# A step order for attention and a gated feed-forward layer on one core: another order of the compute steps, an earlier zeroing, the last output block in three column pieces

## The chip, the core and the metric

The kernel runs on one core of a Trainium2 chip. Five engines work side by side, each through its own list of instructions in order: TensorE (PE) multiplies matrices and writes to PSUM, VectorE (DVE) and ScalarE (ACT) do the elementwise work, GpSimd (POOL) and SyncE (SP) issue most transfers. An instruction starts when the one before it on its engine has gone and the semaphores that it waits for have been counted up. The metric is the device time of one execution in microseconds (us); lower is better.

## What is computed

Block-sparse attention over 32 heads of 768 tokens, then a feed-forward layer with a depthwise convolution as gate. Cut to what matters:

```python
# q, k, v: [4, 8, 768, 64]; mask from blocks of 32 tokens: neighbours, first and last, 3 sampled ones per row
scores = np.where(mask, q @ k.T / 8.0, -1e9)            # per batch and head
attn = softmax(scores)
x = (attn @ v).transpose(0, 2, 1, 3).reshape(4, 768, 512)
h = np.maximum(x @ w_in, 0.0)                            # [4, 768, 1024]
conv_out = sum(conv_w[k] * shifted(h, k - 1) for k in range(3))   # along the tokens
out = (h * sigmoid(conv_out)) @ w_out                    # [4, 768, 512]
```

## The kernel before

**Tiles.** Heads are taken in pairs P = 0 to 15. K and Q of a pair are brought to a transposed slot `t` of 88 rows: 64 rows of the head dimension and 24 rows that carry the block mask, so that one matmul gives masked scores. Pairs 0 to 5 are transposed on PE (`k_tr`, `q_tr`) and copied out of PSUM (`k_cp`, `q_cp`, on DVE or ACT); later pairs are transposed by transfers on SP (`xb`) and copied by `stg_cp`. V gets a column of ones, set by the memsets `v_one`, and is cast or copied by `v_cp`.

**Stages.** The scores are cut into 144 units of eight 128x128 blocks. For each unit there are two `s` steps on PE (L762, into one of two PSUM buffers `st`), one `exp` on ACT (L774, 128x1024, from `st` into one of six buffers `pt`; the first unit's is cut in two halves, so that unit u has `exp.(u+1)` from the second unit on), and two `av` steps on PE (L799, eight matmuls of 65 columns). Counting from 0, unit u has `s.(2u)`, `s.(2u+1)`, `av.(2u)` and `av.(2u+1)`. When a pair's sums are complete, DVE takes the reciprocals and normalises (`rcp`, `norm`, L709), and X is transposed by a transfer (`x_xb`) or on PE (`x_tr`, `x_cp`). Then come x @ w_in on PE (`f1`, L896), `relu` (ACT L916 or DVE L918), the convolution and gate (`mul`, `add`, `g1`, `g2` on DVE, `tanh` on ACT; the last segment's convolution on PE with diagonal weights `diag`), and the second matmul (`f2`, L831), four steps of two matmuls to a block of 128 tokens, an eviction `ev` (ACT L327 or DVE L331) and an output transfer `out` (SP, L840). There are 24 such blocks; the last one (in the function `out_block`, `last`) is computed in column pieces into `st` buffers, which the scores no longer need by then.

**The start.** K, Q and V of pair 0 come as fp32 through the queues of SP and ACT; `cast_q` and `cast_k` bring them to bf16. The mask rows are built on DVE (`a1`, `a3`, `a4`, `a5`, with `ident` from POOL and the sampled blocks from a transfer) and copied into the slot by `m_q0`, `m_k`, `m_h1`, `m_q1`, `m_r1`, and into the other slots by `m_slot`. Until real work is there, PE runs 13 `warm` matmuls of 256 columns on a zeroed tile (`warm_mem`) and 32 `fill` matmuls of 128 columns, which stand at fixed places in its order. `he_zero` sets two edge columns of each of the two h tiles to zero (two memsets each, L364 and L365). The loads of later pairs and of the weights are issued on POOL (L239), held back by one-element `pace` copies.

**What sets the order.** Each step is entered in a graph with its dependences. The text `ORDER` then gives the order in which all steps are put down: two characters are a step's number (base 64), then a letter for its engine where it has a choice (A for ACT, V for DVE), then one character for each buffer that it takes. `put_down` reads it and issues the steps, with `tc.manual_schedule()`. An engine's list is the order in which its steps stand in that text. Costs and due times in the graph are not used when the order is given.

## Time and profile before

| | |
|---|---|
| runs of the kernel before | 207.41, 207.2, 208.66 us; median 207.41 |
| span of the profiled execution (first to last instruction) | 205.4 us |
| instructions | 6237 |
| granted TensorE clock, mean of the span | 1.000 |
| transfers | 25.59 MB, mean 125 GB/s |

The span is counted on the core from the first to the last instruction; the time of a run has some 2 us more around it. Busy times of an engine count each moment once, while the mean length of an instruction is from its start to its end, and neighbours overlap: the distance from one start to the next is what an instruction takes from the engine. A row of the timeline merges neighbours of a kind: start, duration, engine, line, operation, output and input, how many. In brackets stands the idle time before it and what ended it. Some matmul records are missing from the trace.

### The profile page before, as it was taken

The page shows a single profiled execution, that of the slowest core. Times are in us where ns is not written, and L with a number is a line of the kernel's source. Part 1 is how long each engine was busy: PE and PEld are TensorE (multiplying, and loading weights), DVE is VectorE, ACT ScalarE, POOL GpSimd, SP SyncE. Part 2 cuts the span into 40 slices and gives each one's busy share as a digit, 9 for nine tenths or more (in the row PEclk, how much of TensorE's full clock was granted, in tenths as well). Part 3 has the DMA queues.
Part 4 walks back from the last instruction along what each step waited for, and adds up shares of the span by engine and source line. Part 5 has one row for each costly group of instructions (what it writes and reads, how often), then busy time and mean ns, then how long its engine had stood idle before and what let it go on. Part 6 is the DMA issues. An engine that isn't in the chain of part 4 may idle for free.

```text
span 205.4 us, 6237 instructions
## 1 busy us (share of the span) xinstructions
PE 197.1 (96%) x2392; PEld 142.3 (69%) x2409; DVE 184.9 (90%) x572; ACT 189.7 (92%) x253; POOL 59.4 (29%) x113
## 2 busy tenths in 40 slices
PE   7799999999999999999999999999999999999992
PEld 5677877786667766776667767766567667787760
DVE  7999999999999998999899996999999959999960
ACT  6799999999999999999999998999999978998841
POOL 8689255312831133202443253900000000000000
PEclk9999999999999999999999999999999999999999
DMA  5999999994999979999779799998053131000405
GB/s 155 196 190 154 186 178 114 197 127 88 154 150 126 125 103 138 218 166 163 95 105 226 97 117 123 175 154 126 14 174 88 21 123 51 3 2 3 153 3 204
DMA packets 50969, 25.59 MB, mean 125 GB/s; under 512 B 36764, under 2 KB 47996, under 8 KB 50940
## 3 DMA queue, kind: packets, MB, share of 16 engines
q0 software_dynamic: 19728, 11.05, 46.0%
q1 hardware_dynamic: 30924, 13.86, 31.0%
q8 instruction: 19, 0.31, 0.6%
q10 hardware_dynamic: 288, 0.30, 0.5%
q14 instruction: 10, 0.08, 0.1%
HBM read 23.09 MB, written 6.29 MB: 143 GB/s over the span
## 4 chain that ended last, share of the span: by engine, by line
PE 68%; ACT 15%; DVE 12%; issue 3%; ACTq 0%; DVEq 0%
PE st L762 22%; PE mix L896 15%; PE mix L831 15%; PE av L799 12%; ACT pt L774 11%; DVE m L954 3%; DVE t L331 2%; DVE m L962 2%; ACT m L1001 1%; DVE xtok L709 1%; PE st L831 1%; ACT vt L327 1%; DVE diag L379 1%; ACT hE L916 1%; PE mix L728 1%
## 5 line engine op out<-in xcount | busy, mean ns | idle before, releaser
L774 ACT ACTIVATE pt<-st 128x1024 bf16<-128x1024 f32 (+1 forms) x145 | 142.2, 1051 | 4.2 <-PE st L762 3.7
L762 PE MATMUL st<-t 88*128 88x256 bf16 (+2 forms) x600 | 90.5, 267 | 2.3 <-DVE t L331 1.2
L799 PEld LDWEIGHTS <-pt 128*128 128x128 bf16 x1152 | 54.0, 97 | 14.2
L762 PEld LDWEIGHTS <-t 88*128 88x128 bf16 x600 | 48.9, 97 | 21.0 <-issue 1.9
L799 PE MATMUL av<-vt,pt 128*128 128x65 bf16 x1152 | 60.5, 193 | 0.1
L896 PE MATMUL mix<-xT,winb 128*128 128x384 bf16 (+2 forms) x288 | 55.2, 307 | 0.1
L954 DVE TENSOR_SCALAR m<-hE,cw 128x382 bf16<-128x382 bf16 (+2 forms) x192 | 49.1, 312 | 0.4 <-ACT hE L916 0.2
L831 PE MATMUL mix<-woutb,gT 128*128 128x512 bf16 x167 | 47.2, 379 | 0.7
L962 DVE TENSOR_TENSOR m<-m 128x764 bf16<-128x764 bf16 (+2 forms) x64 | 34.1, 532 | 0.6
L896 PEld LDWEIGHTS <-winb 128*128 128x128 bf16 x288 | 24.0, 97 | 9.2 <-issue 0.6
L1001 ACT ACTIVATE m<-m 128x764 bf16<-128x764 bf16 (+2 forms) x32 | 27.1, 853 | 0.0
L831 PEld LDWEIGHTS <-gT 128*128 128x128 bf16 x200 | 17.1, 97 | 10.0 <-DVE gT L1009 1.2
L407 POOL COPY pace<-pt 1x1 bf16<-1x1 bf16 x24 | 6.4, 268 | 54.1 <-ACT pt L774 54.0
L916 ACT ACTIVATE hE<-mix 128x384 bf16<-128x384 f32 (+2 forms) x39 | 19.8, 519 | 0.4 <-PE mix L896 0.2
L1009 DVE TENSOR_TENSOR gT<-m,hE 128x764 bf16<-128x764 bf16 (+3 forms) x36 | 18.2, 509 | 0.4
L709 DVE TENSOR_TENSOR xtok<-av,rcp 128x384 bf16<-128x384 f32 (+2 forms) x36 | 18.3, 507 | 0.4
L239 POOL DMA_DIRECT2D nat<-in_q_dram x23 | 17.3, 752 | 3.8 <-DMA nat<-in_k_dram 1.6
L918 DVE TENSOR_SCALAR hE<-mix 128x384 bf16<-128x384 f32 x25 | 13.7, 553 | 4.3 <-PE mix L896 3.7
L331 DVE COPY t<-mix 64x384 bf16<-64x384 bf16 (+1 forms) x33 | 13.2, 411 | 0.6 <-PE mix L460 0.2
L239 POOL DMA_DIRECT2D nat<-in_k_dram x15 | 12.0, 803 | 3.0 <-issue 2.4
L1004 DVE TENSOR_SCALAR m<-m 128x764 bf16<-128x764 bf16 (+3 forms) x36 | 11.9, 334 | 0.7 <-ACT m L1001 0.7
L327 ACT COPY o2s<-mix 128x512 f32<-128x512 f32 x15 | 9.2, 613 | 3.3 <-PE mix L831 3.2
(76 smaller groups left out, 118.2 us busy)
## 6 DMA issues: line engine op xcount, KB each, us to landing
out_dram<-o2s SPq DMA_DIRECT2D x23, 256.0 KB, 2.2
nat<-in_k_dram POOLq DMA_DIRECT2D x15, 192.0 KB, 4.5
vn<-in_v_dram POOLq DMA_DIRECT2D x15, 192.0 KB, 5.0
nat<-in_q_dram POOLq DMA_DIRECT2D x6, 192.0 KB, 4.5
winb<-in_moe_w_in_dram POOLq DMA_DIRECT2D x2, 512.0 KB, 8.4
woutb<-in_moe_w_out_dram POOLq DMA_DIRECT2D x4, 256.0 KB, 5.8
nat<-in_q_dram POOLq DMA_DIRECT2D x9, 96.0 KB, 5.1
nq<-in_q_dram POOLq DMA_DIRECT2D x6, 96.0 KB, 5.3
```

Of the source, the lines that this page charges most:

```text
L239: return op(name, {eng: occ}, lambda e: on(e).dma_start(out=dst(), in_=src), prio, deps, dma=(kind, service), **kw)
L709: nm = op("norm", {"DVE": t_dps(128 * C)}, lambda e: nc.vector.tensor_tensor(out=xtok_t[xk.index][:, 0:C].rearrange("p c h d -> p h c d"), ...
L762: nc.tensor.matmul(out=st[:, 128 * x:128 * (x + n_)], lhsT=t[0:88, 12 + 6 * hh + kc, :], rhs=t[0:88, idx:idx + (n_ - 1) * (2 if P < NPE el ...
L774: nc.scalar.activation(out=pt_t[ptb.index][:, c0:c1], in_=st_t[stb.index][:, c0:c1], func=AF.Exp, bias=0.0, scale=0.125)
L799: nc.tensor.matmul(out=o[:, off:off + 65], lhsT=pt_t[ptb.index][:, 128 * x:128 * x + 128], rhs=V_t[vslot_b[P].index][:, hh, kc, 0:65], sta ...
L831: nc.tensor.matmul(out=acc(), lhsT=gT_t[gb.index][:, ffc, 128 * t:128 * t + 128], rhs=woutb[:, ffc, c0:c1], start=(ffc == 0), stop=(ffc == ...
L896: nc.tensor.matmul(out=mix_t[hb.index][:, w1 * y:w1 * y + w1], lhsT=winb[:, fc, 128 * ffc:128 * ffc + 128], rhs=xT_t[xt_buf[n].index][:, f ...
L916: nc.scalar.activation(out=dst, in_=src, func=AF.Relu, bias=0.0, scale=0.5)
L954: nc.vector.tensor_scalar(out=m_t[cb.index][:, x, y, 0:w], in0=hE_t[heb.index][:, f0 + y, t0 + x:t0 + x + w], scalar1=cw[:, x, f0 + y:f0 + ...
L962: nc.vector.tensor_tensor(out=m[:, a_, :, 0:w], in0=m[:, a_, :, 0:w], in1=m[:, b_, :, 0:w], op=ALU.add)
L1001: th = [op("tanh", {"ACT": t_act(2 * w) + 0.04}, lambda e, cb=cb, w=w: nc.scalar.activation(out=m_t[cb.index][:, 0, :, 0:w], in_=m_t[cb.in ...
L1009: nc.vector.tensor_tensor(out=gT_t[gtb.index][:, f0:f0 + 2, t0:t1], in0=m_t[cb.index][:, 0, :, 0:w], in1=hE_t[heb.index][:, f0:f0 + 2, 1 + ...
```

## The change

Three things change in the text of the kernel.

1. `ORDER` is another text. All 1,787 steps of the old one are there, with six more (below). 37 steps have another engine, many buffers have another number, and within PE, ACT and DVE most steps stand at another place, by up to 27 places on PE, 8 on ACT and 70 on DVE. On POOL and SP transfers stay within five places of where they were.

Decoded, the beginning of two engines' lists (a digit after the dot counts the steps of a name):

```
DVE before: warm_mem v_one.3 ident_mem a1 nblk v_one.1 a3 ident24 m_k.0 m_h1.1 cast_q.0 a4 v_one.2 v_one.0
            a5.0 q_cp.0 m_q0.1 k_cp.3 cast_q.1 v_one.4 a5.1 m_h1.0 m_q1 m_r1 m_slot.0 k_cp.4 k_cp.5 q_cp.5 q_cp.4
DVE after:  he_zero.0 v_one.3 warm_mem v_one.0 ident_mem a1 nblk ident24 v_one.1 m_k.0 a3 a4
            a5.0 q_cp.0 a5.1 v_one.2 m_h1.1 k_cp.3 m_q1 m_h1.0 v_one.4 m_r1 m_slot.0 v_cp.0 k_cp.4 q_cp.5 k_cp.5
ACT before: m_k.1 cast_k.0 cast_k.1 k_cp.0 m_q0.0 k_cp.1 k_cp.2 exp.0 exp.1 q_cp.1 v_cp.0 exp.2 exp.3 exp.4
ACT after:  m_k.1 cast_q.0 cast_k.0 cast_k.1 k_cp.0 k_cp.1 m_q0.0 m_q0.1 cast_q.1 k_cp.2 exp.0 exp.1 q_cp.1
            exp.2 exp.3 q_cp.4 exp.4
```

On PE, six `fill` stand ahead of the first transpose `k_tr.0` before, one after; `s.0` and `s.1` had 12 `fill` ahead of them and now have 10 and 12, and the rest of the 32 are spread up to `s.16` in both. The steps with another engine:

```
DVE to ACT: cast_q.0 cast_q.1 m_q0.1 q_cp.4 q_cp.11 q_cp.16 relu.9 .11 .16 .18 .20 .24 .32 .39 v_cp.13 ev.15 ev.17 x_cp.7 ev.24
ACT to DVE: v_cp.0 relu.6 .12 .17 .19 .22 .28 .36 .37 .42 ev.1 .4 .6 .7 .21 .23 x_cp.4 x_cp.6
```

On POOL `pace.25` and `ld_win.0` change places, and so do some later paces with their neighbours; on SP some `x_xb` with some `xb`.

2. `he_zero.0`, the zeroing of the edge columns of one h tile, is the first step on DVE (part of the same text). Before, it stood behind the first normalisations.

3. The last output block has three pieces of columns, 256, 128 and 128, in place of two of 256. Each piece has its own four `f2` steps, its eviction and its output transfer, so there are six steps more. The last steps of each engine:

```
PE before:  .. f2.92 f2.96 f2.88 f2.86 f2.93 f2.89 f2.90 f2.94 f2.95 f2.91 f2.97 f2.98 f2.99 f2.87 f2.80 .81 .82 .83
PE after:   .. f2.88 f2.92 f2.96 f2.86 f2.89 f2.97 f2.93 f2.94 f2.98 f2.95 f2.90 f2.91 f2.87 f2.100 f2.99
            f2.101 f2.102 f2.103 f2.80 .81 .82 .83
SP before:  .. out.22 out.24 out.23 out.21 out.20
SP after:   .. out.22 out.24 out.25 out.23 out.21 out.20
```

(`f2.92` to `.95` are the first piece, `f2.96` to `.99` the second, `f2.100` to `.103` the third, which takes the `st` buffer of the first; `ev.20` and `out.20` belong to `f2.80` to `.83`.)

The diff, cut to its first and last lines of `ORDER`:

```diff
 ORDER = """
-000211g010M030405060708090a0S0T1T01U230251262h12j20U0L0O0N0P0Q0R0b0c0d0e0f0g0h0i0j0k0W1e0V0X12V13A17V1AV30Y1CA
...
-q/r0r1A0r2
+0M0L0S1i1g001d021010N0O0U0T03041T00P050W060Q071U080R0X1e090a12V13A2300b0c0d0V1AA10e2521CA0f0Y1DA1E1261K00Z0g1FA0
...
+rF1rL1rs3qQrtrR0r5ruqWrx0rDrGrSryrzrErMqXrNrTqYrOrHrPV0rIr6rJA2rX1rUrYrZrVArKr+qZ1r/VrWr7V3q+s0q/rQr0r8r1A1r2
 """
...
     def out_block(b, t, due, deps, after, tail=False, last=False):
         gb, ob = gt_buf[b], Buf(P_os)
-        halves = ((0, 256), (256, 512)) if last else ((0, 512),)
+        halves = ((0, 256), (256, 384), (384, 512)) if last else ((0, 512),)
...
-                due + 3, [evo], uses=[ob], dma=("hw", 0.65 if not last else 0.4)))
+                due + 3, [evo], uses=[ob], dma=("hw", {512: 0.65, 256: 0.4, 128: 0.25}[c1 - c0])))
```

77 lines of the change are left out of this document (38 added, 39 removed).

## The prediction

> **What bounds the kernel now.** I read the page first, then the busy time by stretch, then the start in order of time.
>
> ```profile
> PE 197.1 (96%) x2392; PEld 142.3 (69%) x2409; DVE 184.9 (90%) x572; ACT 189.7 (92%) x253; POOL 59.4 (29%) x113
> ...
> PE 68%; ACT 15%; DVE 12%; issue 3%; ACTq 0%; DVEq 0%
> ```
>
> Three engines are over 90% busy, and two thirds of the chain that ended last is TensorE (PE). Each row so far is an average, so the stretches come next.
>
> ```profile
> core 0: us, PE busy (x) PEld busy (x) DVE busy (x) ACT busy (x) POOL busy (x), PEclk, DMA share, GB/s
> 7.00:20.00 13.00, 12.37 (x178) 10.09 (x179) 12.40 (x33) 12.80 (x18) 10.47 (x18) 1.00 1.26 174
> 20.00:190.00 170.00, 168.54 (x2083) 121.57 (x2097) 158.72 (x484) 164.91 (x212) 42.74 (x83) 1.00 0.79 119
> ```
>
> From 20 to 190 us PE is busy 168.54 of 170 us: 1.46 us idle. ScalarE (ACT) is idle 5.09 us there and VectorE (DVE) 11.28. So PE bounds this stretch, and no order of the same matmuls can win more than 1.46 us in it. From 7 to 20 us ACT is busy 12.80 of 13 us while PE has gaps: there the exps set the pace. In the long stretch one wait on PE is on record:
>
> ```profile
> PE mix L728 <- DVE xtok L709: 0.3, 1, 0.3
> ```
>
> The 0.3 us are those of a transpose on a normalised block; no step waits for an exp. So what an order can still win lies mostly ahead of 20 us, and what it can lose lies anywhere that PE comes to wait.
>
> What sets the start is seen on DVE, then ACT:
>
> ```profile
> 1.82 0.55 DVE L286 COPY nblk<-ident 24x768 bf16<-24x768 bf16 x1
> ...
> 3.83 0.35 DVE L331 COPY t<-t 24x768 bf16<-24x768 bf16 x1
> ...
> 4.22 0.53 DVE L331 CAST nat<-o2s 128x192 bf16<-128x192 f32 x1
> ...
> 4.78 0.53 DVE L299 SCALAR_TENSOR_TENSOR A<-sbi,keyid,A 24x24 f32<-24x24 int32 x2
> ...
> 5.41 0.12 DVE L359 MEMSET vt<- 128x12 bf16 x2
> ...
> 5.57 0.61 DVE L299 SCALAR_TENSOR_TENSOR mtok<-sbi,keyid,A 24x384 bf16<-24x384 int32 x1
> ...
> 6.59 0.28 DVE L331 COPY t<-mtok 24x128 bf16<-24x128 bf16 x1
> ```
>
> ```profile
> 2.97 0.70 ACT L327 COPY t<-nblk 24x384 bf16<-24x384 bf16 x1
> 3.69 1.07 ACT L327 CAST nat<-o2s 128x384 bf16<-128x384 f32 x2
> 4.67 0.47 ACT L327 COPY t<-mix 64x384 bf16<-64x384 bf16 x1
> 6.21 0.40 ACT L327 COPY t<-mtok 24x256 bf16<-24x256 bf16 x1 [1.08 <-DVE mtok L299]
> 6.64 0.47 ACT L327 COPY t<-mix 64x384 bf16<-64x384 bf16 x1
> 7.29 0.47 ACT L327 COPY t<-av 64x384 bf16<-64x384 bf16 x1 [0.18 <-DVE t L331]
> 7.67 1.07 ACT L774 ACTIVATE pt<-st 128x512 bf16<-128x512 f32 x2
> 8.63 0.47 ACT L327 COPY t<-av 64x384 bf16<-64x384 bf16 x1
> 9.13 0.83 ACT L327 CAST vt<-m 128x768 bf16<-128x768 f32 x1
> 9.87 3.76 ACT L774 ACTIVATE pt<-st 128x1024 bf16<-128x1024 f32 x4
> ```
>
> The columns are start, duration, engine, line and operation. DVE goes without a pause through the casts and the mask to the mask rows `a5.0` (mtok, end 6.18). ACT has stood 1.08 us for them; `m_q0.0` starts at 6.21, and the first exp at 7.67. Then come two half exps, the copy `q_cp.1` and the cast of V, `v_cp.0`; the third exp starts at 9.87, and the exps after it start 0.90 apart ((3.76 − 1.06)/3, with the mean of one exp, 1.06, quoted below).
>
> **The change, part by part.** The start first. Ahead of `a5.0` DVE loses `m_h1.1` (start to next start, 3.83 to 4.22: 0.39), `cast_q.0` (4.22 to 4.78: 0.56) and the two `v_one` memsets (5.41 to 5.57: 0.16). One of those goes to the front (about 0.07), with the zeroing of the edge columns `he_zero.0`, which is two memsets like this:
>
> ```profile
> L364 DVE MEMSET hE<- x2: 65/65/65, 26.1 to 29.9; 128x8 bf16 x2
> ```
>
> Its two lines take 65 ns each, 0.13. Sum: 0.39 + 0.56 + 0.16 − 0.07 − 0.13 = 0.91, so `a5.0` ends near 5.27, if the sampled blocks are there when `a4` wants them at 3.9 instead of 4.78. The trace shows no wait that would bound their landing from below; `cast_k.0`, whose load was issued as early as any, ran unhindered at 3.69, so I take it that up to 0.3 could be lost, hidden by what follows. At the front of DVE the zeroing and one `v_one` delay the zeroed operand of the warm-up matmuls by about 0.2, and ident with it; ident is wanted by `nblk` (start 1.82, perhaps 2.0) and by POOL's first load, which waits behind it on POOL with all later loads, 0.2 each. ACT is shielded by its table load up to 2.97.
>
> ACT now becomes the longer way. After `m_k.1` (end 3.69) stand `cast_q.0` (half the elements of a `cast_k`, so between half of and all of 0.51; I take 0.33), the two `cast_k` (1.07 with overlap, 0.98), `k_cp.0` and `k_cp.1` (a 64x384 copy takes 0.38, 7.29 to 7.67; 0.40 each), `m_q0.0` (6.21 to 6.64: 0.43) and `m_q0.1` (on DVE 0.28; 0.30): 3.69 + 0.33 + 0.98 + 0.80 + 0.43 + 0.30 = 6.53. That is later than the mask rows, so the mask no longer decides. On PE:
>
> ```profile
> 1.06 3.29 PE L230 MATMUL av<-warm 128*128 128x256 bf16 x19 [1.06 <-DVE warm L223]
> ...
> 7.01 0.60 PE L762 MATMUL st<-t 88*128 88x384 bf16 x4 [1.25 <-DVE t L331]
> ```
>
> The first scores step `s.0` started 0.14 after the last row it needs (6.87, the end of `m_q0.1` on DVE) and the exp 0.66 after that. Now 6.53 + 0.14 + 0.66 = 7.33, and ACT is free by 6.53 + 0.33 (`cast_q.1`) + 0.38 (`k_cp.2`) = 7.24. So `exp.0` comes at 7.33 instead of 7.67. The second unit's scores reuse the first PSUM buffer: 7.33 + 0.53 + 0.14 = 8.00 for `s.2`, 0.3 to `s.3` with a filler between, and 0.66: `exp.2` at 8.96, as `v_cp.0` (0.74 on ACT, 9.13 to 9.87) has gone to DVE. Gain 0.9. `q_cp.4` comes to ACT ahead of `exp.4` (0.38). What stays of the lead is 0.9 − 0.4 = **0.5 us**; `v_cp.0` on DVE is behind one `m_slot` copy, about where it ended before, and no exp waits for it while six pt buffers are free.
>
> For the rest of the run the number of steps is the same. 37 small steps change between ACT and DVE:
>
> ```profile
> L916 ACT ACTIVATE hE<-mix 128x384 bf16<-128x384 f32 x31 | 15.8, 524 | 0.1
> ```
>
> A relu is 0.52 on ACT, an eviction 0.58 there (quoted below). To ACT go 8 relu, 3 `q_cp`, 3 evictions; to DVE 9 relu, 6 evictions: ACT's sum behind the first exp falls by about 1 us, DVE's rises by less than 2. Both have idle time in excess of that between 20 and 190 us (5.09 and 11.28), and PE's sum is unmoved, so I cost it at nothing; its cover is PE's own queue, and if that runs dry, what is late is the third rival. On SP, some X transposes change places with K/Q transposes by one or two places; on POOL one pace copy goes ahead of `ld_win.0`, so the first half of w_in is asked for by that copy and its wait later:
>
> ```profile
> L896 PE MATMUL mix<-xT,winb x288: 217/325/328, 28.4 to 193.9; 128*128 128x384 bf16 x112, 128*128 128x256 bf16 x16, 128*128 128x128 bf16 x16
> L239 POOL DMA_DIRECT2D winb<-in_moe_w_in_dram x2: 757/761/765, 15.8 to 19.2; - x2
> ...
> winb<-in_moe_w_in_dram POOLq DMA_DIRECT2D x2, 512.0 KB, 8.4
> ```
>
> The load was issued at 15.8 and the first f1 matmul is at 28.4, 12.6 us apart for a transfer that the page puts at 8.4 to landing: 4.2 to spare.
>
> PE's work between a unit's second scores step and its first av step is what hides the exp. The prices, and the eviction of the last block:
>
> ```profile
> 20.69 0.48 PE av L799 x16
> 21.17 0.44 PE st L762 x4
> ...
> 196.13 0.86 PE mix L831 x4
> ```
>
> ```profile
> L774 ACT ACTIVATE pt<-st 128x1024 bf16<-128x1024 f32 x143 | 141.1, 1057 | 4.2 <-PE st L762 3.7 <-ACT hE L916 0.3
> ...
> L831 PE MATMUL st<-woutb,gT 128*128 128x256 bf16 x16 | 2.4, 272 | 0.0
> ...
> L896 PE MATMUL mix<-xT,winb 128*128 128x128 bf16 x32 | 2.6, 218 | 0.1
> ```
>
> Two scores steps (four matmuls) take 0.44, four av steps (16) 0.48. Counted by these, the old list leaves a mean of 4.3 us of PE work there, the new 3.5. Between unit 20 and unit 140 the old list's tightest are 2.13 to 2.29 and cost nothing in the waits; the new one has four below: units 35, 44, 56 and 60 with 1.84, 1.58, 1.80 and 1.70. An exp that starts at once needs 0.22 for the scores step, 0.16 for its last results (a group of four shows 0.60 where the path has 0.44), 1.06 and two hand-overs (6.18 to 6.21 above is 0.03), about 1.5; one that finds another exp just begun needs 0.90 more, 2.4 at the worst. So each costs between 0 and (2.4 less its cover): together 0 to 2.7. The old list's unit 142 has 1.76 and shows no wait, so I take a value near the low end, **+0.2**.
>
> The last output block: 16 of 256 columns become 8 of 256 and 16 of 128. A 256-column matmul there takes 2.4/16 = 0.150 of busy time, two of 128 take 2 × 2.6/32 = 0.163: 8 × 0.013 = **+0.1**. One more eviction and one more output transfer:
>
> ```profile
> 199.63 0.42 DVE L331 COPY o2s<-st 128x256 f32<-128x256 f32 x1 [1.55 <-PE st L831]
> ...
> 201.01 1.72 SPq L840 DMA_DIRECT2D out_dram<-o2s  x2
> 201.79 0.58 ACT L327 COPY o2s<-mix 128x512 f32<-128x512 f32 x1 [1.14 <-PE mix L831]
> ```
>
> ```profile
> L840 SPq DMA_DIRECT2D out_dram<-o2s x8: 332/362/448, 191.9 to 202.4; - x8
> ```
>
> The third piece reuses the PSUM buffer of the first, whose eviction is 0.42; three f2 steps of 0.43 (0.86 for four matmuls) stand between, so it is hidden with 0.8 to spare. An output issue takes 0.36, and SP stands idle from 201.40 to the last issue at 202.40: it fits. The last step of PE is still a whole 512-column block, its eviction 0.58 and its transfer, so the end after PE is what it was.
>
> Sum: −0.5 + 0.2 + 0.1 = −0.2. The profiled execution has a span of 205.4; the median of the runs is 207.41, 2.0 above, and I take the same difference after: span 205.2, **207.2 us**.
>
> On the clock: the warm-up row shows 19 matmuls in 3.29 us, with starts 0.21 apart for 256 columns, where later 256 columns take 0.11 (1,024 in 0.44). The Trainium skill ("TensorE: Matmul & The Clock Gate", Part 1) says the array starts at half rate and goes to full after about 3.4 us of steady work. By that rule, later and thinner filling speaks against this change, and the sum would be that of rival (b), 207.9, in place of 207.2; the trace agrees that the first 3 us are at half rate, though the granted clock reads 1.00 in every stretch above.
>
> **The rivals.**
> (a) *The start's lead is lost on the way* (loads that land when they did; ACT copies `q_cp.11` and `q_cp.16`, 0.76 together, ahead of unit 30). Against it: no load is waited for by PE in the long stretch. Then +0.2 + 0.1: 207.7.
> (b) *PE stays at the half rate for the first scores steps*, since the warm matmuls start 0.2 later and only one filler, not six, precedes the first transpose. Three s steps ahead of `exp.2` at 0.22 more each: +0.66 on the lead: 207.9.
> (c) *Slower: PE comes to wait for the exp* at the four units above and others with under 2.3 us of cover. For it: PE has no other slack. Against it: unit 142. At the four units' bound: −0.5 + 0.1 + 2.7 = +2.3, 209.7; it ends over 1% slower once all waits sum to 2.5.
> (d) *Faster: the new order also takes most of PE's 1.46 us*, and the whole 0.9 of the start stays: −0.9 − 1.4 + 0.1 = −2.2, 205.2.
>
> **How the numbers follow.** About 1% (2.1 us) is what a measurement of this kernel can tell from no change: its three runs span 207.2 to 208.66. The forecast has 0.47, (a) 0.12, (b) 0.05, (c) 0.23, of which 0.15 with waits over 2.5 us, and (d) 0.13, of which 0.12 below 205.3. That gives 0.12 faster, 0.73 within 1%, 0.15 slower. The range takes (d) on the low side, 205.2, and (c) up to 2.6 us of waits, 209.6.
>
> **What would show it.** Right: first 512-column exp near 7.3, first 1024-column exp near 9.0, ACT without a gap to 20 us, PE busy again over 168 of the 170 us, PE's last matmul to the end of the span unchanged. Wrong: waits of PE av or PE st on ACT exp inside 20 to 190 us (c); starts 0.21 apart for 256 columns behind 4.3 us (b); a first exp no earlier than 7.67, with `m_q0` waiting for the mask still; or an f2 step of the last block that waits for DVE.

## The result and the profile after

The change makes the kernel slower by a little less than 1%. Beside each other on one chip the kernel before took 207.31 us (median of 5 runs) and the changed one 209.29 (median of 5 runs); one of these, of 212.54 us at a granted clock of 0.99, was in a slower state and is left out of the others' range, 208.48 to 209.85, and of the ratio, which is 1.0083, with an interval of 1.0057 to 1.0109. The forecast was 207.2, a ratio of 0.999. The profiled execution of the changed kernel took 209.13 us and has a span of 207.4, against 205.4 before. Lines of kernel.py are one lower than before (L761 is the scores step, L773 the exp, L798 the av step, L830 the f2 step, L326 and L330 the copies on ACT and DVE); in some of the kernels below they are as before.

The page's first part and its chain of waits:

```profile
PE 199.6 (96%) x2397; PEld 143.7 (69%) x2417; DVE 185.7 (90%) x572; ACT 190.4 (92%) x254; POOL 59.4 (29%) x113
...
PE 79%; ACT 9%; DVE 6%; issue 2%; DMA 2%; DVEq 0%; ACTq 0%
```

The share of PE in the chain went from 68% to 79%: the work is still bound by TensorE, more than before. The busy time by stretch (columns as in the prediction):

```profile
7.00:20.00 13.00, 12.41 (x167) 9.94 (x165) 11.08 (x24) 11.62 (x16) 9.07 (x16) 1.00 1.25 169
20.00:190.00 170.00, 168.38 (x2073) 121.07 (x2089) 158.50 (x483) 165.53 (x210) 44.29 (x85) 1.00 0.76 120
```

From 20 to 190 us PE's busy time is what it was (168.38 of 170, before 168.54). What differs in these rows is ahead of it: from 7 to 20 us ACT does 11.62 us of work where it did 12.80. It does less although it was meant to run ahead. ACT in order of time shows where its time went (the brackets name the idle time ahead of a row and what ended it):

```profile
3.94 1.18 ACT L326 CAST nat<-o2s 128x192 bf16<-128x192 f32 x3 [0.27 <-DMA o2s<-in_q_dram]
5.29 0.97 ACT L326 COPY t<-mix 64x384 bf16<-64x384 bf16 x2 [0.18 <-PE mix L459]
...
7.65 1.16 ACT L773 ACTIVATE pt<-st 128x512 bf16<-128x512 f32 x2
8.71 0.47 ACT L326 COPY t<-av 64x384 bf16<-64x384 bf16 x1
9.78 1.02 ACT L773 ACTIVATE pt<-st 128x1024 bf16<-128x1024 f32 x1 [0.60 <-PE st L761]
11.13 1.02 ACT L773 ACTIVATE pt<-st 128x1024 bf16<-128x1024 f32 x1 [0.32 <-PE st L761]
12.44 0.47 ACT L326 COPY t<-mix 64x384 bf16<-64x384 bf16 x1 [0.29 <-DVE t L330]
12.82 5.76 ACT L773 ACTIVATE pt<-st 128x1024 bf16<-128x1024 f32 x6
```

The first exp starts at 7.65 (before 7.67, forecast 7.33) and the first exp of 1024 columns at 9.78 (before 9.87, forecast 8.96). Two waits for scores (0.60 and 0.32) and one of a copy, `q_cp.4` (0.29), stand in these rows, and `exp.4` starts at 12.82 where it started at 11.69. PE in order of time shows why the scores were late:

```profile
1.17 3.06 PE L229 MATMUL av<-warm 128*128 128x256 bf16 x14 [1.17 <-DVE warm L222]
4.75 0.50 PE L459 MATMUL mix<-ident,nat 128*128 128x128 bf16 x3 [0.53 <-ACT nat L326]
...
6.93 0.61 PE L761 MATMUL st<-t 88*128 88x384 bf16 x2
7.33 0.42 PE L229 MATMUL av<-warm 128*128 128x128 bf16 x2
7.54 0.63 PE L761 MATMUL st<-t 88*128 88x256 bf16 x2
...
9.54 0.95 PE L229 MATMUL av<-warm 128*128 128x128 bf16 x7
...
10.93 0.50 PE L459 MATMUL mix<-ident,nat 128*128 128x128 bf16 x6
```

From 7.33 to 7.54 two fillers of 128 columns are issued, 0.105 us each. The six transposes of the same size at 10.93 start 0.055 apart. By the starts of the single matmuls PE ran at half its rate from the first one to 10.5 us, in the kernel before only to 3.9. The column PEclk reads 1.00 in each stretch all the same.

At the end nothing changed but the time at which it comes: the last eviction starts 2.03 us later than before (201.79), with the same 0.58, and the span ends 1.98 later.

```profile
203.82 0.58 ACT L326 COPY o2s<-mix 128x512 f32<-128x512 f32 x1 [1.80 <-PE mix L830]
```

To see where time is lost I compare the start of the n-th exp of 1024 columns or its halves, in order of time and counted from 0, with that of before; the last column is the start of PE's last matmul. In the middle the two orders do their work in another sequence, so that only the early columns and the last one compare like with like between kernels with different orders. All numbers are microseconds after minus before, from one profiled execution each:

```
kernel              2      4     10     15     25     45     55    144   last f2
after           -0.09  +1.13  +1.54  +1.76  +1.78  +1.84  +1.74  +2.14    +2.03
```

Of the 2.0 us, 1.76 seem to be there by `exp.15`, at 23 us. That looks like a loss made at the start alone. It is not: by then the two orders have already done different work on PE. An estimate that compares like with like goes by the work that PE still has to do. Each matmul counts with what its columns take from one start to the next at the full rate in these traces (0.029 us for 65 columns, 0.055 for 128, 0.109 for 256, 0.215 for 512); matmuls whose record is missing are filled in from the weight loads, whose number fits the lists. By that measure the changed kernel is 1.15 us behind at 20 us, 1.45 at 40, 1.74 at 50, 1.65 at 60 and 1.86 at 70, and 2.03 at the last matmul: a little over half of the loss is made ahead of 20 us and the rest behind it. The experiments, too, find a loss in both halves.

### The profile page after: what moved, and what is told of

It reads as the page before. It is cut to its first block, busy times and chain, and to the rows that moved or that the text cites. A ratio compares the mean times of both kernels' runs of the same rounds, so it can differ in the third digit from the quotient of the medians.

```text
span 207.4 us, 6185 instructions
## 1 busy us (share of the span) xinstructions
PE 199.6 (96%) x2397; PEld 143.7 (69%) x2417; DVE 185.7 (90%) x572; ACT 190.4 (92%) x254; POOL 59.4 (29%) x113
## 4 chain that ended last, share of the span: by engine, by line
PE 79%; ACT 9%; DVE 6%; issue 2%; DMA 2%; DVEq 0%; ACTq 0%
PE st L761 25%; PE mix L895 19%; PE mix L830 17%; PE av L798 13%; ACT pt L773 7%; DVE t L330 3%; DMA o2s<-in_q_dram 2%; DVE m L953 1%; PE av L229 1%; PE mix L459 1%; PE st L830 1%; ACT o2s L326 1%; PE av L972 1%; PE mix L727 1%; ACT m L1000 1%
## 5 line engine op out<-in xcount | busy, mean ns | idle before, releaser
L773 ACT ACTIVATE pt<-st 128x1024 bf16<-128x1024 f32 (+1 forms) x145 | 140.6, 1032 | 3.5 <-PE st L761 3.0
L761 PE MATMUL st<-t 88*128 88x256 bf16 (+2 forms) x600 | 92.0, 269 | 1.3 <-ACT pt L773 0.6
L798 PEld LDWEIGHTS <-pt 128*128 128x128 bf16 x1152 | 54.8, 97 | 14.4 <-ACT pt L773 1.0
L761 PEld LDWEIGHTS <-t 88*128 88x128 bf16 x600 | 49.0, 98 | 19.9 <-issue 3.0
L798 PE MATMUL av<-vt,pt 128*128 128x65 bf16 x1152 | 61.6, 193 | 0.2
L830 PE MATMUL mix<-woutb,gT 128*128 128x512 bf16 x164 | 46.4, 379 | 0.7
L830 PEld LDWEIGHTS <-gT 128*128 128x128 bf16 x208 | 17.2, 97 | 10.6 <-DVE gT L1008 1.0
L406 POOL COPY pace<-pt 1x1 bf16<-1x1 bf16 x24 | 7.7, 321 | 56.5 <-ACT pt L773 56.5
L915 ACT ACTIVATE hE<-mix 128x384 bf16<-128x384 f32 (+2 forms) x38 | 18.4, 504 | 0.8 <-PE mix L895 0.4
L330 DVE COPY t<-mix 64x384 bf16<-64x384 bf16 (+1 forms) x30 | 12.3, 418 | 2.1 <-PE mix L459 1.2
L326 ACT COPY o2s<-mix 128x512 f32<-128x512 f32 x12 | 7.2, 602 | 5.6 <-PE mix L830 3.2
L330 DVE COPY t<-stg 64x1536 bf16<-64x1536 bf16 x20 | 11.3, 566 | 0.7 <-DMA stg<-nat 0.4
```

What stands on the lines that cost most here:

```text
L330: nc.vector.tensor_copy(out=dst, in_=src)
L761: nc.tensor.matmul(out=st[:, 128 * x:128 * (x + n_)], lhsT=t[0:88, 12 + 6 * hh + kc, :], rhs=t[0:88, idx:idx + (n_ - 1) * (2 if P < NPE el ...
L773: nc.scalar.activation(out=pt_t[ptb.index][:, c0:c1], in_=st_t[stb.index][:, c0:c1], func=AF.Exp, bias=0.0, scale=0.125)
L798: nc.tensor.matmul(out=o[:, off:off + 65], lhsT=pt_t[ptb.index][:, 128 * x:128 * x + 128], rhs=V_t[vslot_b[P].index][:, hh, kc, 0:65], sta ...
L830: nc.tensor.matmul(out=acc(), lhsT=gT_t[gb.index][:, ffc, 128 * t:128 * t + 128], rhs=woutb[:, ffc, c0:c1], start=(ffc == 0), stop=(ffc == ...
L915: nc.scalar.activation(out=dst, in_=src, func=AF.Relu, bias=0.0, scale=0.5)
```

## The experiments

Eighteen kernels were run. A label with "a" is the changed kernel with something put back or added, one with "b" the kernel before with a part of the change. The orders are lists of step names; the diffs show them by name. Ratios are to the kernel before on the same chip, with their 95% intervals. The matmuls that are added, taken away or repeated in these kernels are warm-up and filler matmuls, which compute nothing that is read.

### What was done alone: zeroing, pieces, warm-up

**b_zero_first**: the kernel before with `he_zero.0` at the front of VectorE.

```diff
 VectorE
+he_zero.0
 warm_mem.0
...
-he_zero.0
 he_zero.1
```

> The old kernel with the zeroing first on DVE and nothing else. Theory 1a: the warm-up starts 0.1 us later, the clock stays at half rate for one or two more windows, and the time is 208 to 209. Theory 1b and theory 2: 207.2 to 207.5, same as before.

Measured: 207.43, ratio 1.0003 (0.9986 to 1.0019). Zeroing first costs nothing.

**b_pieces**: the kernel before with the last block in three column pieces.

```diff
-        halves = ((0, 256), (256, 512)) if last else ((0, 512),)
+        halves = ((0, 256), (256, 384), (384, 512)) if last else ((0, 512),)
```

> The old kernel with the last output block in three column pieces and nothing else. The forecast's price: +0.1 us of PE work and nothing else, 207.3 to 207.6, with the last matmul to the end of the span 4.0 us as before. A rival (the extra eviction or the extra output transfer delays the last one on SP): the time from the last matmul to the end grows by 0.3 or more, 207.7 and up.

Measured: 207.75, ratio 1.0025 (1.0007 to 1.0043), 0.5 us. In its profile the exps stand 0.1 behind before to the end, and PE's last matmul 0.51: about 0.4 is lost among PE's last f2 steps, not behind them, where the second theory had put it. One part of it is a wait for the buffer that the third piece takes over:

```profile
199.16 0.59 PE L830 MATMUL mix<-woutb,gT 128*128 128x512 bf16 x2
199.93 0.61 PE L830 MATMUL st<-woutb,gT 128*128 128x128 bf16 x8 [0.18 <-ACT o2s L326]
```

The eviction that frees the buffer stands behind another on ACT. In the profile of the changed kernel no such wait stands.

**b_cold**: the kernel before without its 13 warm-up and 32 filler matmuls.

```diff
 TensorE
-warm.0 ... warm.12
 k_tr.0
-fill.0 ... fill.31
```

> The old kernel without its 13 warm-up and 32 filler matmuls (their results are read by no one). Theory 1: PE runs at half rate until 10 us or later, the fifth exp comes 1 to 1.7 us later than 11.69, the time is 208.3 to 209.0. Theory 2: the old order's start is carried by DVE and ACT, which the matmuls do not touch: the time stays within 0.3 of 207.3.

Measured: 208.86, ratio 1.0065 (1.0043 to 1.0087). PE stays at half rate to 12.3 us, and the exps stand 0.86 to 0.92 behind before from `exp.4` on, 0.77 by `exp.45`. So not quite a microsecond is what the slow clock costs at this place. In its profiled run a further 1.0 us came at about 59 us, where a transposing transfer landed late; that place comes back below.

### The clock at the start

**a_fill_front**: the changed kernel with five of its fillers put ahead of the first transpose, as many as had stood there before.

```diff
 TensorE
+fill.1 fill.2 fill.3 fill.4 fill.5
 k_tr.0
-fill.1 fill.2 fill.3 fill.4 fill.5
 (their old places, between the transposes)
```

> The new kernel with five of its 32 filler matmuls moved back ahead of the first transpose, where the old list has them; nothing else differs. Theory 1 (clock): in the changed kernel's profile 128-column matmuls start 0.107 us apart until 10.5 us and 0.055 after, because PE stood still from 4.02 to 4.76 and the first busy stretch was too short for the clock to rise; with the fillers back the half rate ends before 5 us, the third exp starts near 9.0 instead of 9.78 and the fifth near 11.2 instead of 12.82, and the time is 207.0 to 207.7. Theory 2 (the steps of the start themselves, or the rest of the order, are what is slow): the time stays at 208.9 to 209.5 even if the rate rises early.

Measured: 209.15, ratio 1.0087 (1.0052 to 1.0121): nothing won. PE still ran at half rate to 10.4 us, and `exp.4` was 1.08 late. Five fillers ahead of the first transpose did not bring the rate up.

**a_zero_back**: the changed kernel with `he_zero.0` where it was, later on VectorE.

```diff
 VectorE
-he_zero.0
 v_one.3
 warm_mem.0
...
+he_zero.0
 he_zero.1
```

> The new kernel with the first zeroing put back behind the first normalisations; the warm-up matmuls can start about 0.1 us earlier. Theory 1a (the clock rises only if a stretch of some 2.8 us of matmuls has been seen by 3.9 us, and the 0.1 us is what was missing): half rate ends near 4 us, time 207.0 to 207.7. Theory 1b (the pause ahead of the first transpose is what keeps the clock down): half rate to 10 us as now, 209.0 to 209.4. Theory 2: 209.0 to 209.4, with no regard to the rate.

Measured: 210.29, ratio 1.0139 (1.011 to 1.0167), slower than the changed kernel. Its profile shows PE at the full rate from 5.2 us, and from 8.7 us at half rate again:

```profile
7.04 0.28 PE L229 MATMUL av<-warm 128*128 128x128 bf16 x2
7.16 0.38 PE L761 MATMUL st<-t 88*128 88x256 bf16 x2
8.60 0.48 PE L499 MATMUL av<-ident,nat 128*64 128x128 bf16 x3 [1.06 <-DVE t L330]
...
9.94 0.95 PE L229 MATMUL av<-warm 128*128 128x128 bf16 x7
```

Two fillers take 0.12 from start to the next start at 7.04, and seven take 0.75 at 9.94 (the next row of PE starts at 10.69). PE had stood idle 1.06 us in between, for a copy on VectorE. The exps fall 2.08 us behind before. So a pause of one microsecond, with thin work before it, went with the loss of the full rate. That a zeroing of 0.13 us, which costs nothing by itself (b_zero_first), should matter so much speaks for the clock's phase and not for the zeroing; with one profile it is argued and not shown.

**a_keep_warm**: nine fillers ahead of the first transpose and sixteen more around the first scores steps.

```diff
 TensorE
+fill.1 ... fill.5, fill.5 three times more
 k_tr.0
...
+fill.9 eight times more
 s.0 s.1
+fill.11 eight times more
 q_tr.1
```

> The new kernel with more filler matmuls where PE stands idle in its start: nine ahead of the first transpose instead of one (five of the 32 moved, three repeated), eight repeated ahead of the first scores step, eight after the second. Theory 1 (clock): the shares of busy time in the 3.4 us windows of the start rise over 0.75, where the runs so far show the rate rise (0.75 to 0.95) and not at 0.65 to 0.70; the half rate ends at 3.5 to 7 us and does not come back, the fifth exp starts at 11.2 to 11.8 instead of 12.82, and the time is 207.0 to 208.0. Theory 2 (the steps of the start as ordered, on ACT and DVE): the rate rises but the fifth exp stays at 12.5 or later and the time at 208.7 or more.

Measured: 209.05, ratio 1.0094 (1.0073 to 1.0116). PE is at the full rate from 5.0 us on and stays there. `exp.2` and `exp.3` start 0.71 and 0.68 ahead of before, which is most of the lead that the forecast had. But `exp.4` is 0.54 behind (1.13 in the changed kernel, so the half rate cost it 0.59), and the total is where it was. ACT in order of time:

```profile
9.15 1.97 ACT L774 ACTIVATE pt<-st 128x1024 bf16<-128x1024 f32 x2
11.85 0.47 ACT L327 COPY t<-mix 64x384 bf16<-64x384 bf16 x1 [0.72 <-DVE t L331]
12.22 2.84 ACT L774 ACTIVATE pt<-st 128x1024 bf16<-128x1024 f32 x3
```

Between the third and fourth exp ACT stands 0.72 us idle, not for an exp's scores but for `q_cp.4`, which the new order puts on ACT. Both halves `q_cp.4` and `q_cp.5` write interleaved columns of one tile, and `q_cp.5` is on VectorE, behind `m_slot.0`, `v_cp.0` and `k_cp.4`; they also read the two halves of one PSUM buffer. `q_cp.4` starts when `q_cp.5` has ended, and everything behind it on ACT waits too. Whether the tile that both write or the buffer that both read sets that order, the trace does not tell.

**a_q_back**: a_keep_warm with `q_cp.4` on VectorE again, behind `q_cp.5`.

```diff
-q_cp.4  ScalarE
+q_cp.4  VectorE
```

> The kernel after with the warm start of a_keep_warm, and q_cp.4 back on VectorE, behind q_cp.5. Theory Q: on ScalarE q_cp.4 waits for q_cp.5, the other copy into the same tile, which VectorE runs behind m_slot.0, v_cp.0 and k_cp.4 (0.72 us of wait in a_keep_warm), and holds exp.4 behind it; with it gone exp.4 starts 0.4 to 0.6 ahead of before's 11.69 instead of 0.54 behind it. Rival P: TensorE brings the scores of exp.4 late (s.7 and s.8 stand behind av.0 to av.4 in the new order); then exp.4 stays 0.3 or more behind. The time is 208.7 to 209.1 by both if what is won at the start is swallowed near 59 us, where the transposes land; 208.0 to 208.4 if it is not.

Measured: 210.75, ratio 1.015 (1.0113 to 1.0187). `exp.4` starts 0.02 ahead of before instead of 0.54 behind. That is between the two theories: of 1.22 us lost between `exp.3` and `exp.4`, 0.52 are still lost; the copy was the larger part, the rest is PE, whose scores are now what the exps wait for:

```profile
11.66 1.02 ACT L774 ACTIVATE pt<-st 128x1024 bf16<-128x1024 f32 x1 [0.39 <-PE st L762]
12.94 3.77 ACT L774 ACTIVATE pt<-st 128x1024 bf16<-128x1024 f32 x4 [0.25 <-PE st L762]
```

And yet the whole is slower than a_keep_warm, by 1.7 us in the medians and by 1.2 in the ratios, and above both of the bands that were expected. A better start with a later end can't be a matter of the start: by the estimate above, 1.4 us of its profiled run go at 59 us and 0.9 between 100 and 120, where PE waits 0.46 us for an X transpose.

### The two halves of the order

**a_start_b_rest**: the new list up to `s.17` (about 18 us), the old list after it, last block in two pieces. **b_start_a_rest**: the old list up to `s.17`, the new one after it, three pieces. **b_rest_two**: the same with two pieces.

```diff
 a_start_b_rest
 new list, steps up to s.17
-new list, remaining steps
+old list, remaining steps
```

```diff
 b_start_a_rest, b_rest_two
-new list, steps up to s.17
+old list, steps up to s.17
 new list, remaining steps
-f2, ev, out of the third piece   (b_rest_two only)
```

> The new list's order and engines up to the second scores step of the ninth unit (160 steps), then the old list, two column pieces. Theories 1 and 2: 208.5 to 209.2. Theory 3: 207.0 to 207.6.

> The old list's order and engines up to the second scores step of the ninth unit (154 steps), then the new list for all that is left, three column pieces included. Both theories that put the loss in the start (1 and 2): 207.3 to 207.9, the last 0.3 being the pieces. Theory 3 (the rest of the new order loses by waits for exps): 208.5 or more.

> Old list to s.17, new list after it, last block in two pieces: b_start_a_rest without the third piece. If the pieces cost the same in either order (0.45), 208.0; if their cost is the wait for st of the older order (0.18) and little else, 208.3; if the rest of the new order were free, 207.4.

Measured: a_start_b_rest 207.81, ratio 1.0035 (1.0017 to 1.0053). b_start_a_rest 208.44, ratio 1.0051 (1.003 to 1.0072). b_rest_two 208.58, ratio 1.0051 (1.0028 to 1.0075). So by the ratios the start alone costs 0.7 us (0.5 in the medians), the rest of the order alone 1.1, and the third piece costs nothing that shows in the new order. The time of each half lies between the bands of the two theories: neither the start nor the rest makes the loss alone. b_rest_two is above all that was expected of it. The rest is the larger part, which the forecast had costed at 0.2.

**a_mended_b_rest**: a_start_b_rest with the fillers of a_keep_warm and `q_cp.4` on VectorE, that is, the new start without its two faults.

```diff
 a_start_b_rest, steps up to s.17
+the 24 repeated or moved fillers of a_keep_warm
-q_cp.4  ScalarE
+q_cp.4  VectorE
```

> a_start_b_rest (207.81: new list up to s.17, old list after it, two pieces) with the warm start of a_keep_warm and q_cp.4 on VectorE, as in a_q_back. If the half clock and q_cp.4 are what made the new start slow, the exps stand 0.3 to 0.4 behind before from unit 5 on instead of 0.95 to 1.36, and the time is 207.3 to 207.6. If the start loses by its order of work as well, 207.7 to 208.0.

Measured: 207.84 beside 207.89 of the kernel before on that chip, ratio 0.9995 (0.9975 to 1.0016). By the ratio the start's loss of 0.35% is gone. The time itself is in the band of the second theory: on that chip 7 of the 19 runs of the kernel before had a granted clock of 0.989 or 0.990 and took longer, 208.07 to 208.53. Against its other 12 runs the mean of the ten is 0.2 us longer. The profiled execution is the fastest of the ten. ACT in order of time:

```profile
7.36 1.07 ACT L774 ACTIVATE pt<-st 128x512 bf16<-128x512 f32 x2
8.32 0.47 ACT L327 COPY t<-av 64x384 bf16<-64x384 bf16 x1
8.86 1.97 ACT L774 ACTIVATE pt<-st 128x1024 bf16<-128x1024 f32 x2
11.23 1.02 ACT L774 ACTIVATE pt<-st 128x1024 bf16<-128x1024 f32 x1 [0.40 <-PE st L762]
12.44 4.77 ACT L774 ACTIVATE pt<-st 128x1024 bf16<-128x1024 f32 x5 [0.19 <-PE st L762]
17.57 1.94 ACT L774 ACTIVATE pt<-st 128x1024 bf16<-128x1024 f32 x2 [0.36 <-PE st L762]
```

The first exp at 7.36 and the first long one at 8.86 are what the forecast had worked out (7.33 and 8.96). Not the mending alone did that: in this execution ACT did not wait for the loaded Q, while a_keep_warm with the same first steps waited 0.23 and had its first exp at 7.64. `exp.4` is 0.45 ahead of before, which is the forecast's lead of 0.5. But three waits for scores, 0.40, 0.19 and 0.36, use it up, and PE's last matmul is 0.08 behind. Even without its faults the new start wins nothing by the end.

**b_vcp**: the kernel before with one part of the new start, the cast `v_cp.0` on VectorE instead of ScalarE, and the first four av steps behind `s.9`.

```diff
-v_cp.0  ScalarE, behind m_h1.0
+v_cp.0  VectorE, behind q_cp.4
 TensorE
-av.0 av.1 ... av.2 av.3
 s.8 s.9
+av.0 av.1 av.2 av.3
```

> The kernel before with one edit of the new start alone: v_cp.0 on VectorE, behind k_cp.4, k_cp.5, q_cp.5 and q_cp.4, and av.0 to av.3 behind s.9. ScalarE is rid of 0.83 us ahead of exp.2: exp.2 and exp.3 start 0.8 earlier, exp.5 0.2 to 0.3 earlier, since s.9 waits for VectorE's copies (done at 11.91 in before). If that lead stays, 207.0 to 207.1; if VectorE, 0.56 us more loaded in a stretch where it is busy 12.40 of 13 us, gives it back, 207.3 to 208.

Measured: 207.85, ratio 1.0024 (1.0003 to 1.0045). `exp.2` to `exp.4` come 0.58 earlier, `exp.6` 0.53 later, and that stays to the end: PE waits 0.38 us for a copy on VectorE and 0.21 for `v_cp.0`, and the exps for PE: VectorE ends the lead, as the second theory had it.

### Where the rest loses

The chain of waits of b_rest_two between 53 and 60 us, in order of time (start, duration, what):

```profile
53.62 4.54 DMA stg<-nat
...
58.25 0.56 DVE t L330
...
59.52 0.39 PE st L761 x2
```

PE's scores wait for a copy, the copy waits for a transposing transfer, `xb.3`. It was issued at 53.62 and landed 4.54 us later. The same place stands in the chain of b_start_a_rest, b_late_two, a_zero_back, b_cold, a_keep_warm and a_q_back; in the last two the transfer took longest:

```profile
53.44 5.54 DMA stg<-nat
```

```profile
53.55 6.76 DMA stg<-nat
```

The queue of SP from 40 us, before:

```profile
40.88 1.18 SPq L718 DMA_TRANSPOSE xT<-xtok  x1
42.16 1.24 SPq L597 DMA_TRANSPOSE stg<-nat  x1
...
48.38 1.28 SPq L597 DMA_TRANSPOSE stg<-nat  x1
49.76 2.52 SPq L718 DMA_TRANSPOSE xT<-xtok  x2
52.37 1.24 SPq L597 DMA_TRANSPOSE stg<-nat  x1
```

and in b_rest_two, whose first 18 us are the same list:

```profile
41.92 1.19 SPq L717 DMA_TRANSPOSE xT<-xtok  x1
43.22 1.24 SPq L596 DMA_TRANSPOSE stg<-nat  x1
...
49.56 1.28 SPq L596 DMA_TRANSPOSE stg<-nat  x1
50.95 2.58 SPq L717 DMA_TRANSPOSE xT<-xtok  x2
53.62 2.67 SPq L596 DMA_TRANSPOSE stg<-nat  x2
```

The whole line moved by 1.0 to 1.3 us, from its first transfer on. That first one, `x_xb.0`, transposes a block that VectorE normalises in `norm.4`. VectorE, before and in b_rest_two:

```profile
40.30 0.55 DVE L709 TENSOR_TENSOR xtok<-av,rcp 128x384 bf16<-128x384 f32 x1
```

```profile
40.88 0.55 DVE L961 TENSOR_TENSOR m<-m 128x764 bf16<-128x764 bf16 x1
41.34 0.56 DVE L708 TENSOR_TENSOR xtok<-av,rcp 128x384 bf16<-128x384 f32 x1
```

`norm.4` keeps its place in VectorE's list, the 97th, but two more `relu` stand ahead of it and two `q_cp` fewer. It starts 1.04 us later, and `x_xb.0` starts when it ends, 1.04 later (40.88 and 41.92). Eight transfers stand on SP between `x_xb.0` and `xb.3`, and up to `xb.3` the two lists on SP are the same. In before the first copy that needs `xb.3` starts at 57.19 with no wait:

```profile
57.19 1.12 DVE L331 COPY t<-stg 64x1536 bf16<-64x1536 bf16 x2
```

In b_rest_two VectorE is ready for that copy at 57.47, 0.3 later, but the transfer, issued 1.25 later, lands at 58.16 (53.62 + 4.54).

What the wait goes with is the room, the time from the issue of `xb.3` to the moment at which VectorE is ready for the copy. Beside it stands how long the transfer took to land, which the traces tell only where it was waited for. These are all kernels that have `xb.3` behind `x_xb.3`:

```
kernel            issued   room   landing after   wait of the copy
b_rest_two         53.62   3.85            4.54   0.8
a_zero_back        55.89   3.87            4.67   0.9
b_cold             53.84   4.09            5.18   1.2
b_late_two         53.55   4.14            4.99   0.9
b_start_a_rest     53.63   4.15            5.07   1.0
b_pieces           52.48   4.75                   0.2
a_fill_front       53.92   4.77                   0
before             52.37   4.79                   0
after              53.85   4.88                   0
a_keep_warm        53.44   4.88            5.54   0.7
b_vcp              52.83   4.92                   0
a_q_back           53.55   4.97            6.76   1.9
a_start_b_rest     53.13   5.06                   0
b_zero_first       51.78   5.25                   0
a_mended_b_rest    51.93   5.59                   0
```

With a room of 4.2 us or less every kernel waits. From 4.75 on only two wait over 0.2 us, and in both the transfer itself took longer, 5.5 and 6.8 us; why, the traces do not settle. So there are two ways to lose here. With the old start and the new rest the line on SP falls behind VectorE's work, and the room shrinks; b_cold, in which the order is the old one throughout, shows that the new order is not needed for that. In the changed kernel everything is late alike, and the room is that of before (4.88 and 4.79): its profile shows no wait. a_keep_warm, which mends half of the start, has that same room; by the estimate of PE's work left it is 0.40 us ahead of the changed kernel at 58 us, and level with it (1.65 behind before) at 60 us, since its transfer took 5.5 us. That is one execution of each kernel.

The same estimate, microseconds behind before, for the kernels on which the argument rests:

```
us in before       20     40     50     58     60     70     90    195
after           +1.15  +1.45  +1.74  +1.69  +1.65  +1.86  +1.86  +1.99
a_keep_warm     +0.56  +1.05  +1.34  +1.29  +1.65  +1.84  +1.84  +1.78
a_start_b_rest  +1.30  +1.03  +1.03  +1.03  +1.03  +1.03  +1.03  +0.75
b_rest_two      -0.13  +0.18  +0.47  +0.42  +0.81  +1.00  +1.00  +0.98
b_rest_xb       -0.19  +0.16  +0.45  +0.40  +0.36  +0.55  +0.91  +0.87
```

In b_rest_two 0.4 us go at the transposes at 59 us. As much as 0.6 goes in smaller pieces ahead of them, 0.2 between 60 and 70 us and 0.2 among the last matmuls (1.21 behind). b_rest_two and b_start_a_rest, whose lists are the same up to the last block, differ by 0.3 us at 40 us (0.18 and 0.51), so pieces of that size are not to be trusted one by one.

**b_late_two**: the old list up to `s.35` (about 24 us), the new one after it, two pieces.

```diff
-new list, steps up to s.35
+old list, steps up to s.35
 new list, remaining steps
```

> Old list up to s.35 (some 24 us) and the new list after it, last block in two pieces: b_rest_two (208.58) with a later change of list. If the rest loses at the transposes near 59 us, which stand on SP behind work that the new order does later, the exps lose nothing up to 25 us and the time is still 208.2 to 208.7. If the loss is made between 15 and 22 us, 207.4 to 207.8.

Measured: 209.12 beside 207.89, ratio 1.0062 (1.0037 to 1.0088), with 0.9 us of VectorE's wait for `xb.3` in its profile. The exps are 0.05 behind up to `exp.11`, but 0.34 from `exp.12` on, at 19 us, where PE's list is still the old one and the expectation had nothing; that is not explained. By the estimate the kernel is 0.3 behind at 24 us and 2.05 at the last matmul: most of the loss is made behind 24 us.

Five kernels then issue `xb.3` ahead of the two X transposes in front of it. ("Unit 55" in these expectations is the column 55 of the first table; the wait of 0.4 us that the second one names is another transfer's, at 123 us.)

```diff
 SP
 xb.2
+xb.3
 x_xb.2
 x_xb.3
-xb.3
```

> b_start_a_rest (208.44, its profiled run 208.87) with one transfer, xb.3, issued on SP ahead of x_xb.2 and x_xb.3 instead of behind them. Theory T: the copy of this transfer at 59 us is what the scores wait for (1.0 us of wait on VectorE, 5.07 us of transfer on the chain of waits); issued 2.5 us earlier it lands in time, the unit 55 stands 0.8 to 0.9 behind before instead of 1.49, and the time is 207.7 to 208.0. Rival: another wait takes its place (the transposes x_xb.2 and x_xb.3, now 1.3 us later, or the work itself): 208.3 to 208.6.

> The kernel after, with xb.3 issued on SP ahead of x_xb.2 and x_xb.3. Its profiled run waited only 0.4 us for this transfer. Theory T (the transfer is a floor near 59 us for all kernels with the new order): 208.5 to 208.9, and the spread of its runs (208.48 to 209.85) shrinks. Rival (the start alone makes after slower): 209.2 to 209.4.

> a_keep_warm (209.05) with xb.3 issued ahead of x_xb.2 and x_xb.3. Theory T: no wait for this transfer near 59 us, unit 55 stands 1.3 to 1.4 behind before instead of 1.72, and the time is 208.3 to 208.6. Rival (another bound holds both): 208.9 to 209.2.

> a_q_back (210.75) with xb.3 issued ahead of x_xb.2 and x_xb.3. Theory T: the 1.9 us that VectorE waited for this transfer go, unit 55 stands 1.5 behind before instead of 2.95, and the time is 208.4 to 209.0. Rival (the transfers are late as a whole, and the next one is waited for instead): 209.8 to 210.8.

> The kernel before, with xb.3 issued ahead of x_xb.2 and x_xb.3. Theory T: before meets the same wait in some of its runs, those of 207.6 to 208.3 (about a quarter); with it gone the median is 207.1 to 207.3 and no run is over 207.6. Rival (the spread comes from elsewhere, or x_xb.2 and x_xb.3, 1.3 us later, are waited for): 207.4 to 207.9, with as many runs over 207.6 as before.

Measured, with the kernel they are derived from:

```
kernel        us      ratio to before            without the edit
b_rest_xb     208.17  1.0046 (1.0022 to 1.007)   b_start_a_rest 208.44
a_xb          209.25  1.0095 (1.006 to 1.0129)   after          209.29
a_warm_xb     209.99  1.0123 (1.0092 to 1.0154)  a_keep_warm    209.05
a_q_back_xb   208.93  1.0075 (1.0053 to 1.0097)  a_q_back       210.75
b_xb          207.49  1.0021 (0.9998 to 1.0044)  before         207.27
```

In none of the five profiles does the copy near 59 us wait any more. Where that wait was longest the time falls: a_q_back_xb is 1.8 us faster than a_q_back in the medians and 1.6 in the ratios. In the others nothing is won clear of the intervals. a_warm_xb is 0.9 us slower in the medians, above both bands, though the intervals of its ratio and that of a_keep_warm overlap; in its profile the X transposes now stand behind `xb.3`, and one of them is waited for:

```profile
PE mix L896 <- DMA xT<-xtok: 0.6, 1, 0.6
```

In a_q_back_xb the same row reads 1.0. In b_rest_xb a copy of the next pair waits for its transfer instead, between 62 and 85 us:

```profile
DVE t L330 <- DMA stg<-nat: 0.8, 1, 0.8
```

So the theory that one transfer holds the new orders back is half right: the line of transposes on SP is one place of the loss, and changing places within it moves the wait to the next one. The traces point at the start of the line, `norm.4`; putting it back was not tried, so that it sets the line's lateness is read from the traces and not shown by a run. b_xb shows nothing won in the kernel before, and its runs spread as before's do (207.09 to 208.95). This transfer is not what makes some of before's runs 0.8 us longer. The record has something that goes with it: of the 106 runs of the kernel before that were taken beside the experiments, 17 had a granted clock of 0.989 or 0.990, and all of these took 208.05 us or more; of the 89 at 0.996 or above, four did.

No kernel beat the one before.

## Why the prediction was wrong

**The bound** was right: PE is busy 168.38 of 170 us from 20 to 190, and no engine took its place. But the busy share does not show what was lost in that stretch. By the estimate of PE's work left some 0.9 us of the loss were made there, and b_rest_two, about 1.1 us slower than before, has PE busy 169.25 of the 170 us, more than before: a matmul counts as busy well past the moment at which the next could start (one of 128 columns shows 0.22 us, and the next starts 0.055 later), and a short wait lies under that.

**The start, −0.5, is the step that failed first.** Its sum "6.53 + 0.14 + 0.66 = 7.33" is right as far as it goes: with the clock up by 4.4 us and Q there in time, a_mended_b_rest has its first exp at 7.36 and its first long exp at 8.86. In the changed kernel three things came between. ACT waited 0.27 for the loaded Q. The forecast put "up to 0.3" on another load, that of the sampled blocks, and took it as hidden; on Q's it put nothing, though ACT had become the longer way. The prices of PE's steps were those of the full rate, and PE was at half rate to 10.5 us. And `q_cp.4` was costed as 0.38 of work on ACT; it also brought a wait for VectorE (0.72 in a_keep_warm, 0.29 in the changed kernel) with the exps queued behind it. The start alone costs 0.7 us where it was to win 0.5; with the two faults mended, nothing by the ratio and 0.2 against the runs of before at the same granted clock; it wins nothing either.

**Rival (b)**, PE at half rate for the first scores steps, was the right mechanism for the clock, given a chance of 0.05 and a price of 0.66. a_keep_warm shows its price in the changed kernel, 0.59 at `exp.4`; b_cold shows 0.9 in the kernel before. The rule of the Trainium skill ("TensorE: Matmul & The Clock Gate", Part 1) spoke for it, and gave a time of 207.9 in that sum. With the row of 0.21 per 256 columns quoted beside it, it deserved more than 0.05. Its time was still 1.4 us short, in part because it left the rest at 0.2.

**The rest, +0.2, is the step that failed most:** 1.1 us by b_rest_two. The forecast looked at PE's cover over the exps, and that term was about right. The changed kernel has four waits of av's weights on exps, 1.0 us together, at units 44, 56, 113 and 142, and a short one at unit 60; 44, 56 and 60 are three of the four units that the forecast had named. Weights load while the matmul ahead of them runs, so PE lost less: by the starts of its matmuls 0.04, 0.14 and 0.12 at units 44, 56 and 60 and nothing to speak of at the other two, 0.3 in all where 0.2 was taken. The sign of rival (c), PE's scores on an exp, is there once, at 49 us:

```profile
PE st L761 <- ACT pt L773: 0.2, 1, 0.2
PEld L798 <- ACT pt L773: 1.0, 4, 0.4
```

("No step waits for an exp" in the old order was true of idle time alone: by the starts, scores came 0.31 and 0.24 us late behind an exp at 72 and 152 us.) What failed is what was costed at nothing. One such step is the sentence on SP, that "some X transposes change places with K/Q transposes by one or two places". It looked at the order on SP, which is unchanged up to `xb.3`, and not at the step on VectorE that releases the first transfer; b_rest_two loses 0.4 us by it at 59 us. In the profile of the changed kernel that place costs nothing, and the 0.9 us behind 20 us are lost in many small pieces. How they divide, and what causes each, stays open: in b_rest_xb the copy near 59 us waits no more, and its profiled run still ends 0.88 behind before.

**The pieces, +0.1,** cost 0.5 in the old order, through a wait for the shared buffer and more besides, and nothing that shows in the new one. That it is "hidden with 0.8 to spare" did not hold in the old order, where the eviction stood behind another on ACT.

**Zeroing first** at nothing, and **the end after PE** unchanged, were right. The start (0.35%) and the rest (0.51%) add up to 0.86%, and the measured loss is 0.83%. But they need not be independent: in the new rest a half-mended start gave nothing back (a_keep_warm).

## What to carry to other kernels

A step that is moved from one engine to another costs its waits as well as its work: ask which other writer of the same tile it now has to wait for, and what is queued behind it. For a queue that issues in order, look up the compute step that releases the first transfer of a run; if that step moves by a microsecond, everything behind it on the queue does, and the price can appear many microseconds later, at a copy that used to find its data there. What counts is the room between the issue and the moment the data is wanted, not the time of the issue. When an early loss is followed by a constant lag, take the early loss away before calling it the cause, and compare two orders by the work still to do, not by the start of the n-th step: here, by that estimate, the start held little more than half of the loss, and PE's busy share showed none of the other half.

## What the runs showed of the hardware that was not expected

The rate of TensorE changed at times that fit windows of a fixed length better than a pause. In a_zero_back it rose at 5.2 us, fell back at 8.65 and rose again at 12.0, so the changes lie 3.5 and 3.4 us apart. Its matmuls filled 75% of the 3.4 us ahead of the first rise, about 40% of those ahead of the fall, in which the longest pause was 1.06 us, and 95% of those ahead of the second rise. In the changed kernel PE stayed at half rate through two stretches of 3.4 us that were filled to about 70% (counted back from the rise at 10.5), and rose after one with about 90%. In the kernel before, the 3.4 us behind the rise, filled to about 40% and holding the pause of 1.25 us, kept the full rate. These shares are worked out from the starts of single matmuls in one run each, so they bound a threshold and do not give one. The Trainium skill ("TensorE: Matmul & The Clock Gate", Part 1) says that a window of about 3.4 us runs freely against the start of the kernel, and that the time of the rise varies by 0.5 us or so. Here the same first steps rose at 3.9, 4.2 and 6.0 us (before, b_pieces, b_rest_two), a wider spread, and with thin work a whole window or two was lost. The profile's row of the granted clock showed none of it.

The page of the kernel before counts 2392 matmuls and 2409 weight loads, that of the changed one 2397 and 2417: 17 and 20 matmul records are missing, all of second matmuls (f2) of 512 columns, and each leaves a gap of 0.05 to 0.13 us that looks like idle time. Sixteen of them, 0.9 us, lie in the 1.46 us of idle time of the long stretch, which the forecast took as what an order could still win there. The other way round, waits that lie under the end of the matmul ahead are not in that figure.
